# Side routing held to its own boundaries, and the last item's rows on one engine, in an attention and two-MoE kernel

## Chip, cores and metric

The kernel runs on one core of a Trainium2 chip. The metric is the device time of one execution in microseconds (us). All instants below are us from the start of the profiled execution's span. The engines are named as in the profile: PE (TensorE), DVE (VectorE), ACT (ScalarE), POOL (GpSimd) and SP (SyncE, which issues most DMAs).

## What is computed

Block-causal attention over 2 batches, 8 heads, 576 positions of 64; its output, read as 1152 rows of 512, goes through two mixtures of experts. Each sends every row to the one of 8 experts with the largest logit.

```
x = attention(q, k, v)                        # 1152 x 512
# MoE 1, for each expert e and its rows:
logits = x @ w_gate; e_idx = argmax(logits); gate_w = softmax(logits)[e_idx]
eom = sigmoid(x @ w_output_gate)
x2[mask] = gate_w[mask] * eom[mask, e] * (relu(x[mask] @ w1[e]) @ w2[e])
# MoE 2: the same on x2 with weights of its own, without eom; an expert
# takes at most `capacity` rows, those beyond it give zeros
```

The weights of an expert are 512 x 1024 and 1024 x 512, in f32.

## The kernel before

**Stages.** Attention runs first, until about 135. Then MoE 1 (class Moe, m = 1), then MoE 2. From the end of attention on, every engine executes its instructions in the order in which the program writes them; what follows is about that order.

**Items.** A MoE is cut into items of up to 128 rows of one expert. Item 0 is made of rows that were ready first, and the others follow from the routing (class Route). The number of items depends on the data: here 10 in MoE 1 (items 0 to 9) and 11 in MoE 2. The program writes items up to NT - 1 = 8 straight; from there on `rest` (L894) opens a branch for each further item, and the Else side holds `finish` (L856). So MoE 1 here passes the branch after item 8 into its body and takes the Else side after item 9.

**An item.** Its rows are gathered (xg), turned on PE and split into a high and a low part (xprep, L602: xh by ACT, xl by DVE). Its weights are loaded into `raw` by SP in chunks of 512 KB; each chunk is cast by ACT (split_hi, wh) and its rest taken by DVE (split_lo, wl). A chunk of raw can be loaded anew when its wl is done. layer1 is 24 matmuls on PE (L618), relu on ACT (hs), htrans turns hs on PE (L1311), hsplit splits it into hh (ACT) and hl (DVE), layer2 is 24 matmuls (L632) into the one bank of PY. store (L634) scales the result by the gate into ys and scatters it with POOL.

**Order of the steps.** `run` (L912) calls layers(s) and go_on(s) in turn. layers(s) (L803): hsplit of item s - 1, layer1 of item s with three hooks between its chunks, four splits of w2, relu, next_a of item s - 2, xprep of item s + 1, tick, layer2 of item s - 1. go_on(s) (L844): two splits, put (yt and nq of item s - 2 on DVE), two splits, htrans of item s, tick, store of item s - 1. finish(s) does the last item's layer2 and begins loading MoE 2's first expert.

**Feeding MoE 2's logits.** While MoE 1 runs, each finished item adds its rows' logits for MoE 2 to lg2: next_a turns ys into yt (transposes L1340), next_b multiplies with the gate's weights (L1358) and DVE writes nr, next_c puts the result at the right rows with nq (L1371), DVE adds it. The last item does so after `run`, with its places (`ready`) made ahead; MoE 2's routing of all rows (step1 and on) comes right behind it.

**The side routing.** The first routing of MoE 2 (route_first, L255) needs only the first NA = 3 tiles of lg2. It runs beside MoE 1's last straight items as a generator: it yields 0 after a small DVE operation and 1 where a product on PE comes next. Class Phases (L396) drives it. `small` gives the small operations one by one until such a boundary; `products` first issues all small operations still open, and then the product with the first step behind it. `tick` (L768) calls products and puts the rest into the list `between`; split_lo calls fill twice, and each fill issues one operation of `between`. A layers or a go_on has four split_lo, so eight fills. The side routing starts in layers(6), where known and the first maximum are issued at once. Then come product one (L266), seven small operations, product two (L297, L299), twenty small operations (kp to rb), product three (L327, L329: the rows and gates of MoE 2's item 0), one step of three operations (ids, io, gs), and fourteen operations from kx to efs. What is still open at the end of `run`'s loop is issued there (L924), before rest(8).

**Buffers.** PX is a ring of four banks of PSUM, used in order by transposes and small products; PR is one bank for the side routing.

The lines that a step rests on:

```python
def products(self):                                   # Phases
    for _ in self.small():
        pass
    if not self.over:
        self.one()
...
    while not self.side.over:                         # run, L924
        self.side.products()
```

Of the kernel before, what the change touches and what calls it, by code (L numbers as in the profile page):

```python
# [31 lines left out]
def kernel(  # L32
# [15 lines left out]
    nc = tc.nc  # L48
    V = nc.vector
    B, H, S, D = q.shape  # L50
    N, DM = out.shape
    E = wg1.shape[1]
    FF = w11.shape[2]
    P = 128
# [26 lines left out]
    ident = const.tile([P, P], F32, name="ident")  # L81
# [562 lines left out]
    class Moe:  # L644
# [121 lines left out]
            self.st["ys"][s] = ys  # L766

        def tick(self):  # L768
            if self.side is not None:
                self.side.products()  # L770
                between.append(self.side.small())

# [30 lines left out]
        def layers(self, s):  # L803
# [27 lines left out]
            if self.side is not None and s == NT - 3:  # L831
                for _ in self.side.small():
                    pass
            g = s - 2
            ga = next_a(R, g, st["ys"].pop(g), late=True) if m == 1 else None
            self.put = lambda: ga()
            if m == 1 and s == 2:
# [18 lines left out]
        def finish(self, s):  # L856
# [20 lines left out]
            self.ws0 = [split(0)]  # L877
            next_c(gb)
            ga = next_a(R, s - 1, st["ys"][s - 1])
            XH.i = XL.i = 0  # L880
            self.xs0 = xprep(xg, PX.next())
# [54 lines left out]
    with ExitStack() as actx:  # L936
# [65 lines left out]
        ready = set()  # L1002
# [175 lines left out]
        last = [None]  # L1178
# [91 lines left out]
    def ring(pool, shape, dt, name, n):  # L1270
        return Ring([pool.tile(shape, dt, name=f"{name}_{i}") for i in range(n)])
# [12 lines left out]
    PX = ring(ps_m, [P, 512], F32, "px", 4)  # L1284
# [46 lines left out]
    def next_places(R, s):  # L1331
        nq, nr = NQ.next(), NR_.next()
        V.tensor_scalar(nq, i128, R.of("pi", s), None, op0=ALU.is_equal)
        nc.gpsimd.tensor_copy(nr[:, :, E], R.of("oht", s))
        return nq, nr

    def next_a(R, s, ys, ready=None, late=False):
        ps = PX.next()
        for c in range(KD):
            nc.tensor.transpose(ps[:, c * P : (c + 1) * P], ys[:, c * P : (c + 1) * P], ident)  # L1340
        yt = YT.next()

        def put():
            if ready is not None:
                nc.scalar.copy(yt[:, 0 : DM // 2], ps[:, 0 : DM // 2])
                V.tensor_copy(yt[:, DM // 2 : DM], ps[:, DM // 2 : DM])
            else:
                V.tensor_copy(yt, ps)
            nq, nr = ready or next_places(R, s)
            return yt, nq, nr  # L1350

        return put if late else put()
# [24 lines left out]
    one = Moe(1, route1, w11, w12, x1d, x2d[:, :])  # L1377
# [15 lines left out]
    one.run()  # L1393

    ready = next_places(route1, "last")
    one.store("last", one.y, True)
    two = Moe(2, route2, w21, w22, x2d, out)
    l1_two = two.first_layer1(one.xs0, one.ws0)
    next(l1_two)
    next(l1_two)  # L1400
    ga = next_a(route1, "last", one.st["ys"]["last"], ready)
    next(l1_two)
    gb = next_b(route1, "last", ga)
# [1 line left out]
    next_c(gb)  # L1405
    two.begin(l1_two, 8, 4, 2, lambda: split_lo(KD + 2))
    two.run()
    two.store("last", two.y, True)


# [28 lines left out]
```

## Time and profile before

| | |
|---|---|
| times of the runs | 453.9, 454.22, 451.9 us (median 453.9) |
| profiled execution | 451.8 us; span from first to last instruction 450.0 us |
| busy share of PE, DVE, ACT, POOL | 92%, 82%, 73%, 22% |
| chain that ended last | PE 70%, DVE 15%, ACT 6%, issue 6% |
| granted TensorE clock, mean | 0.988 |

A timeline's row gives the start, the duration, engine, line, operation, tile written <- tiles read, form and count; in brackets stand the idle time of the engine before it and what ended it. "issue" is idle time for which the profile shows no cause. The chain of waits follows the work that ended last back to its releasers. The granted clock is 1.00 for the full 2.4 GHz. Durations of neighbouring instructions overlap a little, so a start-to-start distance is shorter than a row's duration.

### The profile page before, as it was taken

Reading aid. Unit: us, or ns where it says so; the run is one execution under the profiler, and the core shown is the slowest. Engines: PE = TensorE matmul, PEld = TensorE weight load, DVE = VectorE, ACT = ScalarE, POOL = GpSimd, SP = SyncE. Lnnn points to the kernel's source line nnn. Section 1 sums busy time; section 2 is a strip of 40 time slices with the busy share of each in tenths; the row PEclk is TensorE's granted clock in tenths of the full one; section 3 lists DMA queues with packets and bytes.
Section 4 is the critical chain, followed back from the end, with each engine's and each line's share of the span. In section 5 each row is a group of like instructions: output and inputs, shape, how many; then the busy total and the mean of one; then the engine's idle time right before and its main releaser. Section 6 shows DMA issues by size and latency. Waiting matters only on the chain.

```text
span 450.0 us, 8362 instructions
## 1 busy us (share of the span) xinstructions
PE 414.7 (92%) x2501; PEld 334.0 (74%) x2501; DVE 368.4 (82%) x816; ACT 327.9 (73%) x617; POOL 99.0 (22%) x182
## 2 busy tenths in 40 slices
PE   3899999999988998999997999978989999999993
PEld 2677888877766776788876888755768888888872
DVE  8666776766799999989899796778899999999930
ACT  3678787787775889577868474645959988888930
POOL 8501221121020312033202203102303611111100
PEclk9999999999998999999999899999999999999998
DMA  5567532311074210199519102914628418995000
GB/s 133 110 175 243 133 79 53 82 28 52 20 280 153 72 47 18 32 320 338 194 47 360 63 13 83 348 49 133 259 95 311 146 52 305 395 375 206 24 31 8
DMA packets 58245, 65.99 MB, mean 147 GB/s; under 512 B 34080, under 2 KB 38688, under 8 KB 58180
## 3 DMA queue, kind: packets, MB, share of 16 engines
q1 hardware_dynamic: 54660, 54.62, 37.0%
q0 software_dynamic: 3520, 10.63, 6.8%
q8 instruction: 25, 0.41, 0.4%
q14 instruction: 40, 0.33, 0.2%
HBM read 109.66 MB, written 11.01 MB: 268 GB/s over the span
## 4 chain that ended last, share of the span: by engine, by line
PE 70%; DVE 15%; ACT 6%; issue 6%; DMA 1%; POOLq 0%; POOL 0%; DVEq 0%; ACTq 0%
PE ph L618 21%; PE py L632 20%; PE s L1071 7%; PE pst L1124 6%; PE pst L1098 5%; DVE wl L165 4%; PE px L1311 3%; PE px L605 2%; ACT p L1075 2%; DVE wl_a L165 2%; PE pst L1051 2%; PE px L1358 1%; DVE i128b L99 1%; DVE wl_b L165 1%; PE s L1068 1%
## 5 line engine op out<-in xcount | busy, mean ns | idle before, releaser
L165 DVE TENSOR_TENSOR wl<-raw,wh 128x1024 fp32r<-128x1024 f32 x84 | 98.8, 1217 | 2.6 <-ACT wh L147 2.5
L147 ACT CAST wh<-raw 128x1024 fp32r<-128x1024 f32 x84 | 82.7, 1058 | 1.0 <-DMA raw<-in_moe_w_dram 0.9
L618 PE MATMUL ph<-wh,xh 128*128 128x512 f32 x168 | 69.8, 416 | 2.5 <-ACT xh L607 2.1
L618 PE MATMUL ph<-wl,xh 128*128 128x512 f32 x168 | 67.0, 399 | 1.0 <-DVE wl L165 1.0
L618 PE MATMUL ph<-wh,xl 128*128 128x512 f32 x168 | 67.2, 400 | 0.1
L165 DVE TENSOR_TENSOR wl_a<-raw,wh_a 128x1024 fp32r<-128x1024 f32 x44 | 52.0, 1216 | 0.8 <-ACT wh_a L147 0.3
L147 ACT CAST wh_a<-raw 128x1024 fp32r<-128x1024 f32 x44 | 43.9, 1068 | 7.0 <-DMA raw<-in_moe_w_dram 7.0
L1072 DVE TENSOR_REDUCE mx<-s 128x1 f32<-128x256 f32 (+8 forms) x72 | 34.4, 486 | 17.7 <-PE s L1071 6.2
L165 DVE TENSOR_TENSOR wl_b<-raw,wh_b 128x1024 fp32r<-128x1024 f32 x40 | 47.4, 1219 | 0.9 <-ACT wh_b L147 0.5
L1075 ACT ACTIVATE p<-s,mx 128x256 f32<-128x256 f32 (+8 forms) x72 | 37.8, 527 | 10.0 <-DVE mx L1072 9.0
L147 ACT CAST wh_b<-raw 128x1024 fp32r<-128x1024 f32 x40 | 39.3, 1065 | 0.0
L1098 PE MATMUL pst<-ident,p 128*128 128x128 f32 x200 | 38.6, 286 | 0.4 <-DVE lg L1144 0.3
L618 PEld LDWEIGHTS ph<-wl,xh 128*128 128x128 f32 x168 | 32.1, 191 | 9.2 <-DVE wl L165 3.4
L618 PEld LDWEIGHTS ph<-wh,xh 128*128 128x128 f32 x168 | 31.9, 190 | 8.9 <-ACT xh L607 2.8
L618 PEld LDWEIGHTS ph<-wh,xl 128*128 128x128 f32 x168 | 31.9, 190 | 8.3 <-DVE xl L608 1.7
L632 PE MATMUL py<-wh_a,hh 128*128 128x512 f32 x88 | 35.9, 408 | 0.4 <-ACT hh L1319 0.4
L632 PE MATMUL py<-wh_a,hl 128*128 128x512 f32 x88 | 35.2, 400 | 0.8 <-DVE hl L716 0.5
L632 PE MATMUL py<-wl_a,hh 128*128 128x512 f32 x88 | 35.0, 398 | 0.0
L1302 ACT ACTIVATE hs<-ph 128x512 f32<-128x512 f32 x38 | 22.3, 602 | 16.9 <-PE ph L618 15.5
L641 POOL DMA_INDIRECT x2d<-ys,io x8 | 11.9, 1483 | 95.3 <-ACT ys L640 87.1
L1320 DVE TENSOR_TENSOR hl<-px,hh 128x512 fp32r<-128x512 f32 x38 | 24.4, 681 | 9.9 <-ACT hh L1319 9.9
L632 PE MATMUL py<-wh_b,hh 128*128 128x512 f32 x80 | 32.3, 404 | 0.0
(298 smaller groups left out, 901.5 us busy)
## 6 DMA issues: line engine op xcount, KB each, us to landing
raw<-in_moe_w_dram SPq DMA_DIRECT2D x184, 512.0 KB
out_dram<-zrow SPq DMA_DIRECT2D x9, 256.0 KB
kn<-in_k_dram SPq DMA_DIRECT2D x16, 128.0 KB
qn<-in_q_dram SPq DMA_DIRECT2D x16, 128.0 KB
vn<-in_v_dram SPq DMA_DIRECT2D x16, 128.0 KB
x1d<-x SPq DMA_DIRECT2D x3, 576.0 KB
x2d<-zrow SPq DMA_DIRECT2D x3, 256.0 KB
x1d<-x SPq DMA_DIRECT2D x3, 192.0 KB
```

The source lines that it names most:

```text
L147: nc.scalar.copy(whs[i], raw[:, c, :])
L165: V.tensor_tensor(wls[i], raw[:, c, :], whs[i].bitcast(F32), op=ALU.subtract)
L618: yield nc.tensor.matmul(out_, l[:, c * P : (c + 1) * P], r[:, cols], start=(c == 0 and j == 0), stop=(c == KD - 1 and j == 2))
L632: nc.tensor.matmul(y, l[:, cs], r[:, rs], start=(first and j == 0), stop=(last and j == 2))
L1071: nc.tensor.matmul(ps[:, a:z], s[l][:, b, :], s[r][:, a - o : z - o], start=(j == 0), stop=(j == 2))
L1072: V.tensor_reduce(out=s["mx"][:, t : t + 1], in_=ps[:, o : o + n], op=ALU.max, axis=AX.X, negate=True)
L1075: nc.scalar.activation(s["p"][b][:, 0:n], ps[:, o : o + n], AF.Exp, bias=s["mx"][:, t : t + 1], accum_out=s["sm"][:, t : t + 1])
L1098: last[0] = nc.tensor.transpose(ps[:, j * P : (j + 1) * P], s["p"][b][:, c * P : (c + 1) * P], ident).ins
L1124: nc.tensor.matmul(po[r, 0 : n * BLK], nat["v"][h % NR["v"]][:, c, r], w[:, :, r], start=(c == 0), stop=(c == nc_ - 1))
L1302: nc.scalar.activation(hs[:, i * 512 : (i + 1) * 512], hp[i], AF.Relu)
L1311: nc.tensor.transpose(ps[:, c * P : (c + 1) * P], hs[:, o : o + P], ident)
L1320: V.tensor_tensor(tl, tps[i], th.bitcast(F32), op=ALU.subtract)
```

## The change

Two edits. First, `tick` does something only when the side routing stands at a boundary (at == 1) and is not over. Before, every tick issued all open small operations in a burst and then the next product; now a tick with small operations open passes, they go on through the fills, and the product comes at the first tick that finds them all issued.

Second, the last item of each MoE. `store` is called without `fast`, so ACT alone scales all 512 columns of ys (L640), where ACT and DVE took 256 each (L637, L638). For the last item of MoE 1, next_a (called with `ready`) writes its four transposes into two banks of PX, two in each; ACT copies the first bank's half of yt and DVE the second bank's, where both halves lay in one bank.

```diff
--- before.py
+++ after.py
@@ -766,7 +766,7 @@
             self.st["ys"][s] = ys
 
         def tick(self):
-            if self.side is not None:
+            if self.side is not None and self.side.at == 1 and not self.side.over:
                 self.side.products()
                 between.append(self.side.small())
 
@@ -1335,15 +1335,16 @@
         return nq, nr
 
     def next_a(R, s, ys, ready=None, late=False):
-        ps = PX.next()
+        banks = [PX.next()] * 2 if ready is None else [PX.next(), PX.next()]
+        ps = banks[0]
         for c in range(KD):
-            nc.tensor.transpose(ps[:, c * P : (c + 1) * P], ys[:, c * P : (c + 1) * P], ident)
+            nc.tensor.transpose(banks[c // 2][:, c * P : (c + 1) * P], ys[:, c * P : (c + 1) * P], ident)
         yt = YT.next()
 
         def put():
             if ready is not None:
-                nc.scalar.copy(yt[:, 0 : DM // 2], ps[:, 0 : DM // 2])
-                V.tensor_copy(yt[:, DM // 2 : DM], ps[:, DM // 2 : DM])
+                nc.scalar.copy(yt[:, 0 : DM // 2], banks[0][:, 0 : DM // 2])
+                V.tensor_copy(yt[:, DM // 2 : DM], banks[1][:, DM // 2 : DM])
             else:
                 V.tensor_copy(yt, ps)
             nq, nr = ready or next_places(R, s)
@@ -1393,7 +1394,7 @@
     one.run()
 
     ready = next_places(route1, "last")
-    one.store("last", one.y, True)
+    one.store("last", one.y)
     two = Moe(2, route2, w21, w22, x2d, out)
     l1_two = two.first_layer1(one.xs0, one.ws0)
     next(l1_two)
@@ -1405,7 +1406,7 @@
     next_c(gb)
     two.begin(l1_two, 8, 4, 2, lambda: split_lo(KD + 2))
     two.run()
-    two.store("last", two.y, True)
+    two.store("last", two.y)
 
 
 # ---- launch: one core; inputs and outputs as the reference has them ----
```

## Rows read from the trace of the kernel before

**Rows 1.** The page's busy shares: us (share of the span), instructions

```profile
PE 414.7 (92%) x2501; PEld 334.0 (74%) x2501; DVE 368.4 (82%) x816; ACT 327.9 (73%) x617; POOL 99.0 (22%) x182
```

**Rows 2.** The chain of waits, 222 to 310: start, us, what

```profile
243.37 0.45 PE px L605 x4
...
246.93 7.19 PE py L632 x24
...
262.10 0.44 PE px L605 x4
...
262.53 5.47 PE py L632 x24
...
273.93 0.18 PE px L1371 x2
```

**Rows 3.** PE's timeline, 240 to 264: start, us, instruction [idle before it, releaser]

```profile
246.65 0.21 PE L327 MATMUL pr<-a_ra,a_ohp 128*128 128x5 bf16 x3 [2.84 <-DVE a_ra L320]
```

**Rows 4.** Stages: us; PE, PEld, DVE, ACT, POOL busy; PEclk; DMA share; GB/s

```profile
247.80:250.90 3.10, 3.10 (x9) 2.36 (x8) 3.10 (x5) 0.41 (x1) 0.00 (x0) 0.50 0.19 68
...
250.90:276.40 25.50, 25.50 (x139) 21.73 (x138) 21.65 (x39) 17.54 (x23) 7.37 (x10) 1.00 0.13 42
...
292.60:296.00 3.40, 1.78 (x9) 0.81 (x7) 2.47 (x6) 1.28 (x4) 0.74 (x1) 1.00 0.19 69
```

**Rows 5.** DVE's timeline, 238 to 284

```profile
245.07 0.17 DVE L224 RECIPROCAL a_gate<-a_gate 128x3 f32<-128x3 f32 x1
...
247.18 2.35 DVE L165 TENSOR_TENSOR wl<-raw,wh 128x1024 fp32r<-128x1024 f32 x2
...
255.36 1.29 DVE L1320 TENSOR_TENSOR hl<-px,hh 128x512 fp32r<-128x512 f32 x2 [2.62 <-ACT hh L1319]
...
256.66 0.28 DVE L357 SCALAR_TENSOR_TENSOR a_tx<-a_eo,a_kq,thr 128x72 f32<-128x72 f32 x1
...
263.19 0.69 DVE L608 TENSOR_TENSOR xl<-px,xh 128x512 fp32r<-128x512 f32 x1 [0.63 <-ACT xh L607]
...
263.80 0.14 DVE L382 TENSOR_SCALAR a_dl<-a_ef 128x1 f32<-128x1 f32 x1
...
264.46 2.35 DVE L165 TENSOR_TENSOR wl<-raw,wh 128x1024 fp32r<-128x1024 f32 x2
...
272.12 0.22 DVE L1362 TENSOR_TENSOR nr<-px,oht 128x72 f32<-128x72 f32 x1
...
277.07 0.69 DVE L608 TENSOR_TENSOR xl<-px,xh 128x512 fp32r<-128x512 f32 x1 [1.17 <-ACT xh L607]
...
280.11 0.69 DVE L1348 COPY yt<-px 128x512 f32<-128x512 f32 x1 [2.36 <-issue]
...
283.65 0.30 DVE L1333 TENSOR_SCALAR nq<-i,pi 128x128 f32<-128x128 f32 x1 [2.85 <-issue]
```

**Rows 6.** SP's timeline, 230 to 300: loads issued

```profile
272.23 3.77 SPq L177 DMA_DIRECT2D raw<-in_moe_w_dram  x4
...
278.93 2.54 SPq L175 DMA_DIRECT2D raw<-in_moe_w_dram  x4
```

**Rows 7.** ACT's timeline, 274 to 318

```profile
291.92 1.06 ACT L147 CAST wh_a<-raw 128x1024 fp32r<-128x1024 f32 x1 [0.31 <-DMA raw<-in_moe_w_dram]
292.91 0.47 ACT L637 ACTIVATE ys<-py,last_gs 128x256 f32<-128x256 f32 x1
```

**Rows 8.** DVE's timeline, 274 to 318

```profile
294.50 0.47 DVE L638 TENSOR_SCALAR ys<-py,last_gs 128x256 f32<-128x256 f32 x1
...
295.91 0.42 DVE L1346 COPY yt<-px 128x256 f32<-128x256 f32 x1 [0.93 <-ACT yt L1345]
```

**Rows 9.** Groups by line and shape: busy us, mean ns, idle before

```profile
L640 ACT ACTIVATE ys<-py,gs 128x512 f32<-128x512 f32 x17 | 11.8, 692 | 26.1 <-PE py L632 26.1
```

**Rows 10.** The chain of waits, 425 to 451

```profile
442.74 0.48 ACT ys L637
443.24 0.50 DVE ys L638
```

## The prediction

> **What bounds the kernel now.** I read the profile in this order: busy shares, chain of waits, PE's and DVE's timelines around each place that the diff touches, then the queues of SP and ACT there. The shares [rows 1] name PE, but a share averages over stages; the diff touches three short places, and each is read for itself.
>
> *The side routing.* While MoE 1 runs its items 6 to 8, Phases computes the second MoE's first routing: small VectorE operations, two ahead of each split_lo, and three products on TensorE. In the chain, item 7's xprep ends on PE at 243.82, and layer2 of item 6 starts only at 246.93 [rows 2]. In between stands the third product, in layers(7)'s tick; products() first issues the twelve small operations still open, in a burst. PE's row names them: 2.84 idle, released by a_ra [rows 3]. DVE began them at 245.07, behind xl [rows 5]. The layer2 behind it then takes 7.19 instead of the 5.47 of the next one [rows 2], because the granted clock was 0.50 (1.2 of 2.4 GHz) from 247.8 to 250.9 and 1.00 after it [rows 4]. So this place costs 3.11 of delay, 0.28 of it the product itself, and 1.72 of clock.
>
> *The last item of MoE 1.* ys is scaled half by ACT, half by DVE. ACT's half starts at 292.91, right behind a weight cast [rows 7]; DVE's half starts only at 294.50, behind DVE's own queue, and yt's DVE half at 295.91, having waited for ACT's half [rows 8]. All of MoE 2's routing follows.
>
> *The very end.* The halves of ys run one after the other: 442.74 for 0.48, then 443.24 for 0.50 [rows 10]. Halving one bank's rows between two engines bought nothing here.
>
> **The change, part by part.**
>
> *1. tick only at a boundary (at == 1).* Products one and two stay: the seven operations of phase one fit the eight fills of go_on(6), so the condition holds there as before. Phase two has twenty operations; layers(7) issues eight, and its tick now passes. The other twelve go eight to go_on(7), four to layers(8), and product three goes to layers(8)'s tick.
>
> PE therefore goes from xprep straight to layer2 at 243.82, with no wait, so no clock fall: 3.11 + 1.72 = 4.83 earlier. At layers(8) it pays the product, 0.28. Layer2 of item 7 is then 4.83 - 0.28 = 4.55 earlier than its 262.53 [rows 2].
>
> Does DVE keep up? A small operation costs 0.13 from start to start: twelve from 245.07 to the product at 246.65, five from 263.80 to 264.46 [rows 3, 5]. In go_on(7) DVE ran from 247.18 to 252.74 (hl at 255.36 less its 2.62 of idle) [rows 5], 5.56 with four wl, yt, nq and one small operation. After, it starts at 245.07 with eight small ones: 245.07 + 8 x 0.13 + 5.43 = 251.54. hl's input comes 4.83 earlier, at 250.53, so hl is 1.0 behind PE; the 2.62 of idle is what pays. From hl to the next xl DVE needed 263.19 - 0.63 - 255.36 = 7.20 with eight small operations; with four it needs 6.68 and is free at 258.22. xl's input comes at 263.19 - 4.83 = 258.36. It has just caught up. Product three's last operand follows two hl, one nr, one wl and four small ones: 251.54 + 1.29 + 0.22 + 1.18 + 0.52 = 254.8, while PE arrives at 257.7. No wait.
>
> The price is paid behind that. The loop at the end of run() now issues everything left: ids, io and gs (3), then kx to efs (14): 17 operations, where five stood before [rows 5]. 17 x 0.13 = 2.21. They stand in DVE's queue ahead of go_on(8)'s four wl, yt, nq, hl and nr. xl ends at 258.97, the burst at 261.18, against wl's 264.46: DVE is only 3.28 ahead of the old time where PE is 4.55 ahead. Call the gap L = 1.27. Bounds for the twelve added operations: nothing, if they hide completely (L = 0), and 0.28 each for all 17, the longest such row [rows 5], which makes 4.76 and L = 4.76 - 0.66 - 0.28 = 3.82. I take 0.13 because two stretches of the same mix of dependent and independent operations agree on it. (The Trainium skill, "VectorE: DVE Perf Modes", section "The TRN2 errata", gives an operation between SBUF tiles 58 cycles and one for each element at 0.96 GHz; as an estimate for 28 elements, the mean here, that is 0.09 each, a burst of 1.5 and a gain 0.7 larger than the sum below. The rows read 0.13, since dependent operations don't overlap, and the sum goes by them.)
>
> Who waits for a late DVE? PE's next_c in layers(9): nr ends at 272.34, next_c starts at 273.93, so 1.59 of cover [rows 2, 5]; L is inside it. The next xl has 1.17 of idle [rows 5]: used up, 0.1 left over, not charged. SP is not covered: its last conditional load waits for the last wl_b, ends at 276.00, and the load of MoE 2's first weights follows at 278.93 [rows 6]. Both move with DVE, by 3.28.
>
> *2. Last item's rows on ACT alone, two banks.* ACT's cast ahead of ys is fed by those loads and moves by 3.28, so ys starts at 292.91 - 3.28 = 289.63 and takes 0.69 [rows 7, 9]. Four transposes, 0.44 as xprep's [rows 2], end at 290.8. DVE's half of yt no longer waits for ACT's half (another bank) nor DVE's ys half; it takes the slot of that half: 294.50 instead of 295.91, 1.41 earlier, then 3.28 more: 291.22. ACT's half lies beside it. The extra bank moves every later use of the four-bank ring by one; the distance between uses stays four, so I cost it at nothing; cover is that rk is read out long before its bank returns.
>
> MoE 2's routing thus starts 3.28 + 1.41 = 4.69 earlier, and the rest follows from it: routing, loads, gathers, and then PE.
>
> *3. The end.* From 442.74 to the end of DVE's half is 1.00; one ACT row of 0.69 and a hand-over of 0.02 take its place: 0.29 [rows 9, 10]. The scatter behind it is unchanged.
>
> **Sum**: gain = 4.55 - L + 1.41 + 0.29 = 6.25 - L = 4.98. The profiled execution took 451.8 (its span 450.0): 446.8. It is the fastest of those shown; the median is 453.9 (451.9 to 454.22). Since the removed stall is in every execution, I take the gain from the median: 448.9. Bounds: 6.25 from 451.9 gives 445.7; 2.43 from 454.2 gives 451.8.
>
> **The rivals.**
>
> *The stall moves with the product.* If product three still finds its operands missing in layers(8), the 4.83 are lost there again and only 1.41 + 0.29 stay: 452.2. For it: DVE is 1.0 behind at hl. Against: the margin of 2.9 worked out above. 0.13.
>
> *The clock falls elsewhere.* At the end of MoE 1 PE now waits in one piece for the whole of ys, some 2 us, where before it waited in two. In the old stretch from 292.6 to 296.0 PE was busy for 1.78 of 3.40 and the clock stayed at 1.00, while 2.84 in one piece were followed by a fall [rows 3, 4]. Two lies between. A fall costs 1.72 at most: 450.6. 0.12.
>
> *Slower: DVE's instruction stream runs dry at the branch.* After the jump of rest(9) DVE idles 2.36 ahead of yt and 2.85 ahead of nq, for nothing the profile shows [rows 5]; at the branch of rest(8), behind the five operations, wl follows with no gap. If DVE, arriving late with seventeen short operations, shows those two gaps there too, and the operations cost their upper bound, L = 3.82 + 5.21 = 9.03, and the gain is 6.25 - 9.03 = -2.8: 456.7. It decides from L = 6.25. Against: that branch was passed without a gap. The Trainium skill, "Runtime: NRT & Kernel Launch", section Instruction fetch mechanics, says that a taken branch whose target is not at hand waits for a fetch; by that rule the gap belongs to the jump of rest(9), which stays, and the trace agrees in that only there DVE shows it. 0.04.
>
> **How the numbers follow.** Forecast 448.9 with 0.71. A measurement of this kernel tells about 0.5%, 2.3 us, from no change. Faster by more: the forecast and the clock rival, 0.83; within: the moved stall, 0.13; slower: 0.04. The range leaves out little but the last two cases: 446.0 to 451.7.
>
> **What would show it.** Right: no idle ahead of L327's matmul, its row ahead of layer2 of item 7, about 258; layer2 of item 6 in 5.5 with the clock at 1.00; a burst of some 2.2 between xl and wl on DVE; SP's L175 near 275.7; one ACT row of 128x512 for ys, then DVE's yt without a wait for ACT's. Wrong: PE waiting for nr in layers(9), an idle "issue" on DVE at rest(8), or ys on ACT waiting for a cast that waits for DMA by more than it did.

## The result and the profile after

The changed kernel takes 448.08 us, the median of 12 runs (445.67 to 451.31), beside 454.11 for the kernel before in the same session (12 runs, 451.66 to 456.07). The ratio is 0.990, with a 95% interval from 0.987 to 0.992: 4.7 us faster, somewhere between 3.5 and 5.9. Forecast were 4.98 us and 448.9. The profiled execution took 449.08, its span is 447.4. That is only 2.6 under the span of before, in part for a reason that lies ahead of the change and is told below. Runs more than 1.5% above the fastest of their kernel, three in this whole study, are left out of every comparison.

The first view is the page: busy shares, and the granted clock in tenths in 40 slices of the span.

```profile
PE 416.8 (93%) x2501; PEld 335.6 (75%) x2501; DVE 368.2 (82%) x814; ACT 328.6 (73%) x617; POOL 97.6 (22%) x182
PEclk9999999999996999999999999969999999999998
```

The shares are those of before [rows 1] but for a point; nothing of the change shows in them. The clock's line shows more: two slices of this execution stand at 6. One is at the end of attention, some 100 us ahead of the first changed instruction. Behind it, when layer2 of item 5 begins, which both kernels do alike, this execution is 1.41 later than the profiled one of before (230.92 against 229.51); 0.26 of it was there at 136, ahead of that fall. All comparisons below are therefore made from the start of that layer2.

PE's timeline from 240 to 262, as start, us, instruction (many rows of layer 1 and layer 2 are left out):

```profile
244.62 0.60 PE L605 MATMUL px<-ident,xg 128*128 128x128 f32 x4
244.98 0.47 PE L632 MATMUL py<-wh_a,hh 128*128 128x512 f32 x1
...
250.53 1.03 PE L1311 MATMUL px<-ident,hs 128*128 128x128 f32 x8
...
258.50 0.60 PE L605 MATMUL px<-ident,xg 128*128 128x128 f32 x4
258.94 0.22 PE L327 MATMUL pr<-a_ra,a_ohp 128*128 128x5 bf16 x3
259.02 0.21 PE L329 MATMUL pr<-a_rb,a_ohp 128*128 128x2 bf16 x3
259.09 0.48 PE L632 MATMUL py<-wh_b,hh 128*128 128x512 f32 x1
```

xprep of item 7 (L605) is followed at once by layer2 of item 6 (L632), which takes 5.55, from 244.98 to 250.53. The wait of 2.84 [rows 3] and the layer2 of 7.19 [rows 2] are gone. The third product (L327) stands ahead of layer2 of item 7 and waits for nothing: no bracket behind its row.

The same stretch by stages (us; busy time of PE, PEld, DVE, ACT, POOL; granted clock; DMA share; GB/s), and the stretch after the last item:

```profile
243.80:249.30 5.50, 5.50 (x30) 4.64 (x29) 5.09 (x12) 5.19 (x7) 0.00 (x0) 1.00 0.99 374
249.30:272.00 22.70, 22.55 (x127) 18.94 (x126) 21.97 (x51) 16.79 (x22) 7.39 (x10) 1.00 0.13 46
292.00:296.00 4.00, 3.84 (x19) 2.82 (x16) 2.09 (x9) 2.52 (x4) 1.06 (x1) 0.72 0.18 69
296.00:300.00 4.00, 4.00 (x20) 2.91 (x19) 3.97 (x21) 0.60 (x1) 0.00 (x0) 0.50 0.00 0
```

The clock stays at 1.00 (2.4 GHz) where it had been 0.50 (1.2 GHz) for 3.1 us [rows 4]. In its place it falls from 292 on, where before it stayed up.

DVE's timeline, where the price was to be paid:

```profile
259.76 0.69 DVE L608 TENSOR_TENSOR xl<-px,xh 128x512 fp32r<-128x512 f32 x1 [0.49 <-ACT xh L607]
260.37 0.15 DVE L332 CAST a_ids<-pr 128x1 int32<-128x1 f32 x1
...
262.77 0.15 DVE L392 COPY a_efs<-a_ef 128x1 f32<-128x1 f32 x1
262.84 2.35 DVE L165 TENSOR_TENSOR wl<-raw,wh 128x1024 fp32r<-128x1024 f32 x2
...
270.50 0.23 DVE L1363 TENSOR_TENSOR nr<-px,oht 128x72 f32<-128x72 f32 x1
...
277.16 0.69 DVE L1349 COPY yt<-px 128x512 f32<-128x512 f32 x1 [2.22 <-issue]
279.53 0.29 DVE L1333 TENSOR_SCALAR nq<-i,pi 128x128 f32<-128x128 f32 x1 [1.68 <-issue]
```

The 17 operations, from a_ids to a_efs, take 2.47 from 260.37 to wl at 262.84. wl follows with no idle time; the two idle pieces named "issue" stand where they stood before, behind the jump of rest(9) [rows 5].

PE's and SP's timelines behind that:

```profile
270.34 0.39 PE L618 MATMUL ph<-wh,xl 128*128 128x512 f32 x1
270.87 0.42 PE L1372 MATMUL px<-nr,nq 128*128 128x81 f32 x2
```

```profile
277.39 2.20 SPq L175 DMA_DIRECT2D raw<-in_moe_w_dram  x4
```

PE's matmuls follow each other by 0.23 here, so next_c, 0.53 behind the last one, came 0.3 late: it waited for nr. SP's load of MoE 2's first weights starts 46.47 behind the common point, against 49.42 before [rows 6].

The last item of MoE 1, ACT's rows, then DVE's:

```profile
289.89 1.05 ACT L147 CAST wh_a<-raw 128x1024 fp32r<-128x1024 f32 x1 [0.32 <-DMA raw<-in_moe_w_dram]
290.84 0.68 ACT L640 ACTIVATE ys<-py,last_gs 128x512 f32<-128x512 f32 x1
292.05 0.37 ACT L1346 COPY yt<-px 128x256 f32<-128x256 f32 x1 [0.53 <-PE px L1341]
```

```profile
292.11 0.28 DVE L1333 TENSOR_SCALAR nq<-i,last_pi 128x128 f32<-128x128 f32 x1
292.30 0.42 DVE L1347 COPY yt<-px 128x256 f32<-128x256 f32 x1
```

One row of ys, and DVE's half of yt 1.46 after its start, where it had been 3.00 [rows 7, 8], with no wait for ACT's half.

The end of the chain of waits:

```profile
440.42 0.70 ACT ys L640
441.12 0.03 POOLq L641
```

From the start of ys to the scatter's issue 0.70 stand where 1.00 stood [rows 10].

From start to start, counted from layer2 of item 5, the two profiles and a second profile of the changed kernel (a run below) give, in us:

| | before | after | again | earlier |
|---|---|---|---|---|
| layer2 of item 7 | 32.78 | 28.17 | 28.17 | 4.61, 4.61 |
| layer2 of item 8 | 46.66 | 42.43 | 42.42 | 4.23, 4.24 |
| SP's load for MoE 2 | 49.42 | 46.47 | 46.57 | 2.95, 2.85 |
| ys of the last item | 63.40 | 59.92 | 60.38 | 3.48, 3.02 |
| its yt, DVE's half | 66.40 | 61.38 | 61.85 | 5.02, 4.55 |
| second matmul of layer2, MoE 2's item 0 | 78.21 | 73.61 | 74.06 | 4.60, 4.15 |
| last ys | 213.23 | 209.50 | 209.80 | 3.73, 3.43 |

So 4.6 or 4.2 of gain enter MoE 2. Some 0.8 of it (0.87 and 0.72) goes again inside MoE 2, where a load is in the chain of waits near 326 in both kernels. The piece of the chain before, then after:

```profile
328.86 3.94 DMA raw<-in_moe_w_dram
```

```profile
325.68 4.79 DMA raw<-in_moe_w_dram
```

It is 0.85 longer; that this load is what takes the 0.8 back is read from place and size, and no run isolates it.

With the 0.30 at the very end, 1.41 of late start in the one and what MoE 2 took back, the spans differ by 2.6 (4.60 - 0.87 + 0.30 - 1.41). Executions differ in the clock falls ahead of the change; the medians of many runs say 4.7.

### The profile page after: what moved, and what is told of

Its sections match the earlier page's. It is cut to its first block, busy times and chain, and to the rows that moved or that the text cites. A ratio compares the mean times of both kernels' runs of the same rounds, so it can differ in the third digit from the quotient of the medians.

```text
span 447.4 us, 8359 instructions
## 1 busy us (share of the span) xinstructions
PE 416.8 (93%) x2501; PEld 335.6 (75%) x2501; DVE 368.2 (82%) x814; ACT 328.6 (73%) x617; POOL 97.6 (22%) x182
## 5 line engine op out<-in xcount | busy, mean ns | idle before, releaser
L618 PE MATMUL ph<-wh,xh 128*128 128x512 f32 x168 | 70.9, 422 | 2.8 <-ACT xh L607 2.1
L618 PE MATMUL ph<-wl,xh 128*128 128x512 f32 x168 | 68.4, 407 | 1.0 <-DVE wl L165 1.0
L618 PE MATMUL ph<-wh,xl 128*128 128x512 f32 x168 | 68.5, 407 | 0.1
L632 PE MATMUL py<-wh_a,hh 128*128 128x512 f32 x88 | 35.4, 402 | 0.4 <-ACT hh L1319 0.4
L632 PE MATMUL py<-wh_a,hl 128*128 128x512 f32 x88 | 34.5, 392 | 0.3 <-DVE hl L1320 0.3
L632 PE MATMUL py<-wl_a,hh 128*128 128x512 f32 x88 | 34.4, 391 | 0.0
L632 PE MATMUL py<-wh_b,hh 128*128 128x512 f32 x80 | 32.3, 404 | 0.0
L1124 PE MATMUL pst<-tp,vn 128*64 128x128 f32 (+2 forms) x384 | 31.9, 289 | 0.0
L632 PE MATMUL py<-wh_b,hl 128*128 128x512 f32 x80 | 31.3, 391 | 0.5 <-DVE hl L1320 0.5
```

Source lines behind the costliest of these rows:

```text
L618: yield nc.tensor.matmul(out_, l[:, c * P : (c + 1) * P], r[:, cols], start=(c == 0 and j == 0), stop=(c == KD - 1 and j == 2))
L632: nc.tensor.matmul(y, l[:, cs], r[:, rs], start=(first and j == 0), stop=(last and j == 2))
L1124: nc.tensor.matmul(po[r, 0 : n * BLK], nat["v"][h % NR["v"]][:, c, r], w[:, :, r], start=(c == 0), stop=(c == nc_ - 1))
```

## The experiments

The theory: the stall belongs to the tick, the last item's rows and banks are a second and independent gain, and the price is the burst on DVE. The rivals that matter are the clock (its term could be an accident of the execution, and it could fall at the end of MoE 1 instead) and the burst (it could cost nothing, or more). The diffs are against the changed kernel unless the text says against before. No run leaves out any of the computation; the transposes and small operations that three of them add aren't used by it.

**The tick alone** (against before):

```diff
-            if self.side is not None:
+            if self.side is not None and self.side.at == 1 and not self.side.over:
```

> The first edit alone (tick passes while small operations are open); store and next_a of the last item as before. If the stall in layers(7) and the clock fall behind it carry the gain, and DVE's burst at the end of run's loop gives part of it back by way of SP's loads: layer2 of item 6 follows xprep with no wait and takes 5.5, the loads of MoE 2 start some 3.0 earlier than before (beside whatever the executions differ in before 243), and the time is 3.0 us (2.3 to 3.5) under before. If the last item carried the gain: less than 1 us. If DVE bounds all of MoE 1, so that PE only waits elsewhere: PE shows new waits of some 3 us in items 7 to 9, and the gain is under 1 us.

Measured: 449.11, ratio 0.9915 (0.9881 to 0.9949), 3.9 faster; the interval, 2.3 to 5.4, holds the expected 3.0. In PE's timeline the product stands behind xprep of item 8 with no wait:

```profile
255.57 0.60 PE L605 MATMUL px<-ident,xg 128*128 128x128 f32 x4
256.01 0.22 PE L327 MATMUL pr<-a_ra,a_ohp 128*128 128x5 bf16 x3
```

Layer2 of items 7 and 8 begin 28.17 and 42.42 behind layer2 of item 5: the changed kernel's values to 0.01. So these 4.6 and 4.2 belong to the tick alone.

**The last item alone** (the changed kernel with the old tick):

```diff
-            if self.side is not None and self.side.at == 1 and not self.side.over:
+            if self.side is not None:
```

> The second edit alone (ys of the last item by ACT alone, yt through two banks); tick as before. If the terms of the sum hold: yt's DVE half 1.4 earlier against the start of ys than before, 0.3 at the end, so 1.7 us (1.2 to 2.0) under before. If the last item carried the gain: 3 us and more. If its chain is covered by DMA or DVE work anyway: 0.3 us.

Measured: 450.54, ratio 0.9942 (0.9915 to 0.9969), 2.6 faster, with 1.7 expected inside the interval. The stall is back, to the hundredth (the row below), while the yt of the last item starts 1.59 behind ys, against 3.00 before and 1.46 in the changed kernel:

```profile
245.02 0.21 PE L327 MATMUL pr<-a_ra,a_ohp 128*128 128x5 bf16 x3 [2.84 <-DVE a_ra L320]
```

The two parts give 3.9 and 2.6, together 6.5, and both at once 4.7 to 4.9. The three intervals are wide enough for the parts simply to add; the runs don't show that they do. Nor does the profile of this run show the 2.6: in it the clock falls from 280 to 288 (0.91, 0.66), ys waits for layer2 and starts 1.44 later than in before, and yt no earlier (66.43 against 66.40). The time rests on the runs alone, and they lost less to the clock too (6.9 against 8.9, by the measure used below).

**One bank** (the changed kernel, its transposes in one bank):

```diff
-        banks = [PX.next()] * 2 if ready is None else [PX.next(), PX.next()]
+        banks = [PX.next()] * 2
```

> The changed kernel with both halves of yt in one bank again, ys still by ACT alone. If the gain at the last item comes from ACT taking all of ys, and DVE's half of yt stands behind DVE's own queue in any case: yt's DVE half starts 0.35 us later relative to ys, and the time is 0.3 us above the changed kernel, too little for the runs. If the two banks carry it: DVE's half starts 1 us and more later, and the time is 1.0 to 1.4 above.

Measured: 448.54, ratio 0.9885 (0.9851 to 0.9918), the changed kernel's time. DVE's timeline shows the wait for ACT's half come back:

```profile
293.43 0.42 DVE L1347 COPY yt<-px 128x256 f32<-128x256 f32 x1 [3.01 <-ACT yt L1346]
```

It starts 1.84 behind ys (291.59), against 1.44 to 1.59 in the eight profiles with two banks. So of the 1.5 that this part of the change is worth, the second bank gives 0.25 to 0.4; a time of that size can't be told from none in the runs, and the row tells it. The other 1.2 belongs to scaling on ACT alone, but not wherever ys is scaled: before, DVE's half of ys stood 1.59 behind ACT's because of DVE's own queue [rows 7, 8]. Where that queue was empty, in the run that fills the wait of before (below), the two halves started 0.51 apart and yt came 1.93 behind ys, in one bank. There ACT alone is worth 0.1. (In this run, too, ys came late, by 3.9 and 3.4 against the changed kernel's two profiles, behind a clock of 0.50 from 284 to 288.)

**The burst doubled** (17 operations more behind it):

```diff
                 while between:
                     fill()
+                pad = route_pool.tile([P, E], F32, name="pad")
+                V.memset(pad, 0.0)
+                for _ in range(16):
+                    V.tensor_scalar_add(pad, pad, 1.0)
```

> The changed kernel with 17 more small operations on DVE behind the burst, ahead of go_on(8): L grows by 2.2 to 3.8 (each 0.13, or up to 0.2 since each depends on the one before: 3.4). If DVE's lateness there is paid in full through nr and the loads of MoE 2: wl of go_on(8) and SP's first load come 2.2 to 3.4 later relative to layer2 of item 7, PE waits about as long ahead of next_c in layers(9), and the time is 2.2 to 3.4 us above the changed kernel (more by 1.7 if the clock falls behind that wait). If DVE has slack enough there: no more than 0.5 us.

Measured: 450.94, ratio 0.9949 (0.993 to 0.9967): 2.3 faster than before, 2.6 slower than the changed kernel beside it. The pad on DVE, and PE's stages behind it:

```profile
259.85 0.07 DVE L929 MEMSET pad<- 128x8 f32 x1
259.95 3.26 DVE L931 TENSOR_SCALAR pad<-pad 128x8 f32<-128x8 f32 x16
263.23 2.40 DVE L165 TENSOR_TENSOR wl<-raw,wh 128x1024 fp32r<-128x1024 f32 x2
```

```profile
264.00:268.00 4.00, 3.14 (x13) 2.57 (x14) 4.00 (x6) 3.26 (x4) 3.51 (x5) 0.77 0.17 66
268.00:272.00 4.00, 4.00 (x10) 3.13 (x11) 4.00 (x6) 0.00 (x0) 0.76 (x2) 0.50 0.25 66
```

The pad costs 3.38. SP's load for MoE 2 comes 50.07 behind the common point instead of 46.57 in the changed kernel's second profile, 3.50 later. So DVE sets the pace of the loads, as the sum said: what the burst takes, SP's loads lose in full. PE now waits 1.66, for wl in layer1 of item 9 and not ahead of next_c as expected, and the clock falls to 0.50 in a place where it falls in no other profile. With both, layer2 of item 8 begins 5.2 later; ys, 3.8 later, here waits for the last layer2 (0.29) and no longer for the cast that the loads feed.

**The burst spread** (a third small operation ahead of each split_lo from layers(7) to layers(8), and one stop less in the side routing, so that the product goes to the tick of go_on(7)):

```diff
     i = c + s * KD
-        fill()
-        fill()
+        for _ in range(2 + more[0]):
+            fill()
...
         r["gs"] = gs
-        yield 1
+        yield 1 if m == 1 else 0
...
+                more[0] = int(self.m == 1 and s >= NT - 2)
                 self.layers(s)
```

> The changed kernel, with three small operations ahead of each split_lo instead of two from layers(7) to layers(8), and no stop between ids and kx. Product three then comes in go_on(7)'s tick, behind htrans, and only 3 of the 17 operations are left for the burst ahead of go_on(8). If the burst's lateness of DVE (L, 1.6 in the trace of the changed kernel) costs its full length by way of SP's loads: wl of go_on(8) and those loads come 1.2 earlier relative to layer2 of item 7, and the time is 1.2 us (0.7 to 1.6) under the changed kernel, 5.9 under before. If DVE is only moved and what counts is its total: as the changed kernel within 0.4. If product three now waits for its operands on PE in go_on(7): a PE wait there of up to 1 us, and nothing gained.

Measured: 449.35, ratio 0.9883 (0.9854 to 0.9912). The rows moved as expected: three operations are left of the burst, and SP's load comes 45.45 behind the common point, 1.0 earlier than in the changed kernel; next_c no longer waits.

```profile
260.35 0.15 DVE L393 COPY a_efs<-a_ef 128x1 f32<-128x1 f32 x1
260.42 2.35 DVE L166 TENSOR_TENSOR wl<-raw,wh 128x1024 fp32r<-128x1024 f32 x2
```

```profile
274.96 2.52 SPq L176 DMA_DIRECT2D raw<-in_moe_w_dram  x4
```

The time is not told apart from the changed kernel's (by the ratios it is 0.4 to 0.6 less, where 1.2 was expected), so alone this run shows no gain in time. Its profile says why the earlier load can fail to pay. The clock fell to 0.61 from 280 to 284, the last layer2 ended later, and ys waited for it and not for the cast behind the load; it starts 60.84 behind the common point, later than in the changed kernel (59.92 and 60.38):

```profile
290.35 0.69 ACT L641 ACTIVATE ys<-py,last_gs 128x512 f32<-128x512 f32 x1 [0.98 <-PE py L633]
```

**Filling the wait of before** (against before: 24 transposes of ident ahead of the third product):

```diff
             if self.side is not None:
+                self.ticks = getattr(self, "ticks", 0) + 1
+                if self.ticks == 3:
+                    idle = PX.next()
+                    for j in range(24):
+                        nc.tensor.transpose(idle[:, j % 4 * P : (j % 4 + 1) * P], ident, ident)
                 self.side.products()
```

> The kernel before, with 24 transposes of the identity into a bank of PX ahead of product three in layers(7): PE works through the 2.8 us in which it waited; their result is not used. The delay stays, only PE's activity differs. If the clock falls because of that wait: the granted clock stays at 1.00 from 247 to 251, layer2 of item 6 starts as late as before and takes 5.5 instead of 7.2, and the time is 1.7 us (1.2 to 2.0) under before. If the clock fall belongs to something else (DMA, a load peak): it falls all the same, and the time is as before. If DVE bounds the stretch, the 1.7 come back as PE waits in layers(8), and the time is as before.

Measured: 455.12, ratio 1.0018 (0.999 to 1.0047): no gain, where 1.7 was expected. At the stall itself the run did what it should. PE's timeline and the stage behind it:

```profile
242.22 2.78 PE L774 MATMUL px<-ident 128*128 128x128 f32 x24
245.22 0.21 PE L327 MATMUL pr<-a_ra,a_ohp 128*128 128x5 bf16 x3 [0.22 <-DVE a_ra L320]
```

```profile
247.80:250.90 3.10, 3.10 (x15) 2.54 (x14) 3.10 (x5) 0.00 (x0) 0.00 (x0) 1.00 0.00 0
...
284.00:288.00 4.00, 4.00 (x15) 3.42 (x13) 1.35 (x3) 3.38 (x5) 0.00 (x0) 0.50 1.03 393
288.00:292.00 4.00, 4.00 (x12) 3.29 (x12) 3.31 (x4) 2.04 (x3) 0.00 (x0) 0.50 0.52 198
```

There the clock stays at 1.00, and layer2 of item 7 begins 31.18 behind the common point, not 32.78: 1.60 won on the spot, and layer2 of item 8 is still 1.60 earlier, so DVE didn't take it back in layers(8). But 35 us later the clock stands at 0.50 for some 8 us, where in before it was 1.00, and ys of the last item starts 3.7 later than in before. Over 11 runs it loses 10.8 us to the clock on average (span times one less the mean granted clock), and before, beside it, loses 8.9. A fall of the clock that is prevented in one place is thus no gain to count on: the next one may come elsewhere. A fall from 280 on stands in three profiles without this filling too, so the filling didn't have to cause it; why the later falls cost more here stays open.

**Filling the wait for ys** (12 transposes of ident ahead of next_a of the last item):

```diff
     next(l1_two)
+    idle = PX.next()
+    for j in range(12):
+        nc.tensor.transpose(idle[:, j % 4 * P : (j % 4 + 1) * P], ident, ident)
     ga = next_a(route1, "last", one.st["ys"]["last"], ready)
```

> The changed kernel with 12 transposes of the identity on PE ahead of next_a of the last item, in the 1.4 us in which PE waits for ys; their result is not used. If that wait makes the clock fall and the fall costs time: clock 1.00 for the 8 us behind ys, and 0.4 us (0.2 to 1.7) under the changed kernel. If the falls only move to the next wait, as in the filled layers(7): the mean clock over the runs is no better than the changed kernel's 0.984 and the time is the same or up to 1 us longer.

Measured: 448.54, ratio 0.9896 (0.9859 to 0.9934), no difference. PE's timeline says why little can be read from it:

```profile
288.06 1.47 PE L1404 MATMUL px<-ident 128*128 128x128 f32 x12
291.12 0.65 PE L1341 MATMUL px<-ident,ys 128*128 128x128 f32 x4 [1.59 <-ACT ys L640]
```

The transposes ended at 289.53, and PE still waited 1.59 in one piece, as long as without them (1.43 and 1.12), since ys came later here (61.62 behind the common point; its cast waited for its load). So the run didn't remove the wait. The clock fell from 292 on (0.67).

**The changed kernel again**, beside the three runs above that were made in one session with it:

> The changed kernel once more, beside the next three and as their reference. Expected: 4.7 us (3.5 to 6.0) under before; layer2 of item 6 follows xprep without a wait at a clock of 1.00. If the clock falls come at other places in every execution, the falls of this profile stand elsewhere than in the first one (137 to 143 and 294 to 301), while layers(7) stays free of one.

Measured: 448.37, ratio 0.9892 (0.9868 to 0.9917). Its profile repeats the terms of the sum (the table above) and shows a fall at 292 to 296 once more, at 0.57. One at 180 to 184 (0.59), ahead of the common point, is new.

**The wait for ys taken away.** In the profile after, ACT's last cast ahead of ys waits for its DMA until 289.89, while layer2's last matmul had started at 289.30. This run moves that cast, and its subtraction on DVE, behind ys into the start of MoE 2:

```diff
-                if f in (3, 5):
-                    split(KD + f // 2 - 1)
+                if f == 3:
+                    split(KD)
...
-    two.begin(l1_two, 8, 4, 2, lambda: split_lo(KD + 2))
+    two.begin(l1_two, 8, 4, 1, lambda: split_lo(KD + 1))
```

> The changed kernel, with the last of the two weight casts that stand ahead of the last item's ys on ScalarE (it waited for its DMA until 289.89 in the changed kernel's profile, and ys started at 290.84 although layer2 had ended near 289.5) moved behind it, into the start of MoE 2; its subtraction on VectorE goes with it. All of the work is still done. Theory (TensorE's wait for ys is what the clock falls behind at the end of MoE 1): ys starts some 1.2 earlier after layer2 of item 5 than in the changed kernel (59.9 and 60.4 in two profiles, so about 58.9), TensorE waits about 0.75 for it instead of 1.1 to 1.4, the granted clock stays 1.00 from 292 to 300, the first ohx comes about 1.2 earlier, and the time is 1.2 to 1.6 under the changed kernel's 448.4. Rival (the moved cast and subtraction are paid at the start of MoE 2, where VectorE's chain of small operations sets the pace): ohx 1.2 earlier but the first layer2 of MoE 2 not, and the time the same. A fall of the clock in 288 to 300 all the same would say that a wait of 0.75 is enough for it, or that it isn't the wait.

Measured: 447.62, ratio 0.9864 (0.9822 to 0.9906). That is under the changed kernel by 0.8 in the medians and by 1.3 in the ratios, each taken against before of its own session, with 1.2 to 1.6 expected: too little to be told from it. ACT's row, PE's row and the stage behind:

```profile
288.45 0.69 ACT L640 ACTIVATE ys<-py,last_gs 128x512 f32<-128x512 f32 x1 [0.43 <-PE py L632]
```

```profile
289.19 0.73 PE L1341 MATMUL px<-ident,ys 128*128 128x128 f32 x4 [0.45 <-ACT ys L640]
```

```profile
292.00:296.00 4.00, 3.88 (x20) 2.83 (x20) 3.75 (x16) 1.20 (x2) 0.00 (x0) 0.57 0.00 0
```

ys starts 58.92 behind the common point (58.9 expected), the first ohx 63.89 (65.62 in the changed kernel's second profile), and the second matmul of MoE 2's first layer2 72.34 against 74.06: 1.7 earlier, and kept where MoE 2 begins. Its rival, that the moved work is paid there, falls. At the end of MoE 2 nothing of the 1.7 is left in this profile: the last ys starts at 210.04, against 209.50 and 209.80, and on the way the clock stood at 0.65 from 332 to 336, where the changed kernel's two profiles have 1.00. And the clock falls to 0.57 from 292 on all the same, behind a wait of 0.45. So a longer wait for ys isn't needed for that fall.

**Both** (the spread burst and the later cast together):

> The run with the burst spread over earlier fills, with the moved cast of the run beside it added. If both gains are real and independent: weights loaded for MoE 2's first item 1.0 earlier after layer2 of item 5 than in the changed kernel (45.4 against 46.5), ys up to 1.0 earlier again where the loads feed the casts ahead of it (about 58), and the time 1.5 to 2.5 under the changed kernel's 448.4, about 446.4. If the loads that stand behind these (the DMAs of MoE 2's first items) set the pace, as in the changed kernel's chain of waits near 320 to 330, the time stays within 1 of 448.4.

Measured: 446.00, ratio 0.9836 (0.9798 to 0.9875), 7.4 under before and 2.4 under the changed kernel, as expected (446.4). SP's load stands at 45.81 behind the common point (0.7 earlier, 1.0 expected), ys at 58.53, layer2's second matmul of MoE 2 at 71.95, 2.1 earlier than in the changed kernel's second profile.

```profile
275.32 2.21 SPq L176 DMA_DIRECT2D raw<-in_moe_w_dram  x4
```

It is the fastest kernel of this study. Its interval and the changed kernel's just overlap (it ends at 0.9875, and the changed kernel's two begin at 0.9868 and 0.987), so that it beats before is shown, and that it beats the changed kernel is likely.

## Why the prediction was right, point by point

*The stall goes and doesn't come back.* Right. 4.55 was forecast at layer2 of item 7, and 4.61 came; the nine profiles with the new tick have that layer2 between 28.15 and 28.18 behind the common point. The rival that the stall moves with the product had a margin of 2.9 against it (3.2 came: DVE's last operand was done at 255.73, the product started at 258.94); no row of L327 behind the new tick has a wait.

*The gap L.* Mechanism right, size under. The burst took 2.47 for 17 operations, 0.145 each, not 0.13. DVE was 4.61 - 3.03 = 1.58 behind PE, where 3.03 is what wl gained from the common point (34.95 to 31.92); forecast was 1.27. That next_c wouldn't wait was wrong. The cover of 1.59 was read from the chain, where next_c begins at 273.93; PE's timeline of before has it earlier:

```profile
273.77 0.34 PE L1371 MATMUL px<-nr,nq 128*128 128x81 f32 x2
```

So the cover was 1.43, and 0.14 of it is the hand-over from nr to PE: 1.29 against 1.58, which is the 0.3 of waiting. The doubled burst shows the slope: 3.38 more on DVE, 3.50 at SP, 2.6 in the time. (The estimate that the prediction made from the Trainium skill, "VectorE: DVE Perf Modes", section "The TRN2 errata", was 1.5 for the burst; the section itself calls that formula too short for a single operation. The row reads 2.47; each of the 16 dependent operations of the pad, 128x8, took 0.20. The measurement decides.)

*SP's loads.* 3.28 forecast, 2.95 and 2.85 measured: L's error again. That ys follows them holds in both profiles of the changed kernel, where its cast waits for a load; in the runs whose clock falls between 280 and 292 ys waits for PE instead.

*The last item.* ys to yt was to shrink by 1.41 and shrank by 1.54 and 1.53. yt came 5.02 and 4.55 earlier, with 4.69 forecast. Most of it is ACT's, and only because DVE was busy when ys came (see the run with one bank). The end gave 0.30 for 0.29.

*The clock term of 1.72, inside the 4.55.* Right in the place, and weaker than the prediction took it for. The fall stands in both profiles that have the stall (before and the run of the last item alone) and in none of the nine that have neither stall nor filling. But the run that filled the wait won the 1.60 on the spot and no time. The loss to the clock over a whole run (span times one less its mean granted clock) is 8.84 on average in 45 runs of before and 7.4 in 18 of the changed kernel, which fits a lasting gain of 1.5; the run of the last item alone, though, which keeps the stall, has 6.9 in 11. So how much of the 1.72 lasts is open. The 3.11 of delay doesn't hang on it.

*The clock rival.* It named the place, and the cause that it gave doesn't cover what the runs show. The clock did fall at the end of MoE 1 in both profiles of the changed kernel. But it fell there too in the run of the tick alone, whose ys is in two pieces as before (0.57 from 292 to 296), and with the wait cut to 0.45 it fell still. It stayed at 1.00 from 292 to 296 in the runs of the last item alone, of the spread burst and of the doubled burst; there PE, late itself, waited only 0.45 for ys too, and the clock had fallen earlier, between 264 and 288. A wait in one piece of 1.1 to 1.6 was followed by a fall in all three profiles that have one, so it may be enough; it isn't needed. Nor was the price 1.72: in the second profile yt was 4.55 earlier and MoE 2's first layer2 4.15, so 0.4; in the first 5.02 and 4.60, again 0.4. From yt to that layer2 it takes 11.81 to 11.88 in the six profiles whose clock is above 0.9 from 292 to 296, and 11.91 to 12.23 in the other six: DVE's small operations are most of the chain there, and a slow PE beside them is mostly hidden. Nor is 1.72 the most that a fall can cost: where the wait of before was filled, 1.6 ahead at layer2 of item 8 became 3.7 behind at ys, over the fall from 280 on. What makes the clock fall there stays open.

*DVE's stream running dry at rest(8).* Fell: wl follows a_efs with no idle. (The Trainium skill, "Runtime: NRT & Kernel Launch", section Instruction fetch mechanics, has a taken branch wait for a fetch when its target is not at hand. The trace agrees again in that, of the two branches, DVE idles only behind the jump of rest(9), 2.22 and 1.68; no run shows a fetch.)

*The number.* 4.98 was forecast, and the ratio says 4.7 (3.5 to 5.9). No term of the sum was off by more than 0.31 (L's), and what ys to yt gained beyond its term, 0.13, makes up for part of that. What the sum left out is what MoE 2 took back, 0.8 in the profiles: "the rest follows from it" was not so. By the two profiles the gain is 4.60 - 0.87 + 0.30 = 4.03 and 4.15 - 0.72 + 0.30 = 3.73. So the parts are right, and that the whole came out within 0.3 of the runs' 4.7 is in part luck: what an execution loses to the clock differs by more than that, from 4.0 to 9.0 in 18 runs of the changed kernel.

## What to carry to other kernels

A product put at a fixed point drags every small operation that it needs to that point, in one burst on an engine that others wait for; put it where its operands have come anyway, and look at once for where the leftover operations then pile up. Here the pile met a slack of some 1.3 on PE and cost it 0.3, but it cost the loads that wait for DVE its full length; spread, it let those loads start 1.0 earlier, which the time alone didn't show. Cost delay and clock as separate terms, and trust the delay: the clock's share of a stall can come back at another place. And before a row is taken from a busy engine, see whether it was the splitting or the queue that it waited for: here it was the queue.

## What the hardware showed that was not expected

The clock's falls move. Twenty-four transposes kept it at 1.00 through a stall that had cost it 3.1 us at 0.50, and the same execution then had some 8 us at 0.50 in a stretch, 284 to 292, where before had 1.00. In the twelve profiles falls stand in five stretches between 240 and 344 (244 to 252, 264 to 276, 280 to 292, 292 to 308, 332 to 344). Falls stood behind waits of PE of 2.84, 1.66, 1.43, 1.12 and 0.45, and other waits, of 0.45 and of 1.16, had none behind them, the two pieces at the end of MoE 1 in before among them [rows 4].

A dependent VectorE operation of 8 elements for each partition took 0.20 from start to start (16 in 3.26), while the mix of dependent and independent ones in the burst took 0.145. The burst's first three, which read pr and not each other, start at 260.37, 260.43 and 260.50.
